# When the attention of a gated mix asks for VectorE time, and when the weight sums of one FFN chunk are formed

## The chip, the cores and the metric

The kernel runs on one core of one Trainium2 chip, with the matmuls on TensorE (PE), sums and products on VectorE (DVE), copies and exponentials on ScalarE (ACT), accumulating transfers issued by GpSimd (POOL) and most other transfers by SyncE (SP). The metric is the device time of one execution in microseconds, lower is better. Times are medians of several executions.

## The reference

```python
def _A_ref(x, wqkv, wo):          # S 2048, D 512, H 32, Dh 16
    W, dil = 8, 2
    qkv = (x @ wqkv).reshape(B, S, 3, H, Dh)           # then split into q, k, v by head
    idx = pos[:, None] - (arange(W) * dil)[None, :]    # eight keys, two apart, none before 0
    logits = where(idx >= 0, einsum(q, k[idx]) * Dh ** -0.5, -1e9)
    return einsum(softmax(logits), v[idx]).reshape(B, S, D) @ wo

def _B_ref(x, w_gate, w_up, w_down):                   # F 1792
    return (gelu(x @ w_gate) * (x @ w_up)) @ w_down

g = sigmoid((x * gate_w).sum(-1, keepdims=True))
return g * _A_ref(x, wqkv, wo) + (1 - g) * _B_ref(x, w_gate, w_up, w_down)
```

All data are float32. A token of even number needs only even tokens for its attention, and one of odd number only odd ones.

## The kernel before

The tokens are handled in two halves by parity, `par` 0 and `par` 1, each of 1024 tokens in eight tiles of 128 (`jj` 0 to 7). Every matrix operand is split into a rounded part and a remainder (`hi`, `lo`), and a product takes three matmuls: high by high, remainder by high, high by remainder.

For a half the stages are: `project(par, 0)` makes the first half of the keys and queries, `project(par, 1)` the values, `ffn(par)` the FFN in `FC` = 14 chunks of 128 hidden channels. For `par` 0 the first projection is written out by hand at the start. The second half of the keys and queries is made inside the first FFN chunks: `project_one(par, jj)` makes one tile (12 matmuls), tiles 0 to 5 in chunk 0, tiles 6 and 7 in chunk 1. From chunk 2 on, a chunk has four tiles of the down projection in the same places (`down`, six matmuls each, for the pair of chunks before); the last pair's eight down tiles stand behind the chunks, in the tail of `ffn`.

A chunk multiplies by a fast scheme with seven products of six matmuls each instead of eight (`product`, L480), on sums of activation blocks (`sums_x`) and sums of weight blocks. The weight sums of chunk f are formed by `combine(f)` on VectorE (three subtractions, L423) in the buffer `raw` that `fetch(f)` filled (`raw` has two buffers). `operands` makes from them, for two groups of products, the two parts: ScalarE writes the negated rounded part (L441), a GpSimd transfer adds the raw value to it in place (L442), and ScalarE writes the rounded part (L446). `down_w` does the same for the down weights (L470, L471, L473). For `par` 1 the parts of the first group come back from DRAM, where `keep` and `keep_parts` stored them. `gate_up` writes out the order of one chunk: steps `idle(0)` to `idle(8)` between its products and the four `pieces`; the dictionary `do` holds what is called at a step, filled by `at(step, function, ...)`, and `late` carries a chunk's last product into the next chunk.

Attention is work for VectorE, 128 channels (a unit `u`, four of them a half) at a time. The generator `attention()` yields the price in us of each step that it has emitted: `scores` (four pairs of a product L288 and a reduction L291, 2.3 each), `softmax`, `mix` (four times a product L326, sums L330 to L334, two transposes L339 that go to DRAM). It is asked by `pull(budget)`: the budget is added to a credit, and steps are emitted while the credit is above zero. So the numbers in the calls of `pull` say how much attention stands beside which matmuls:

```python
def idle(i, n):
    for x in do.get(i, ()):
        x()
    pull(n * PACE[par] * (1.0 if par or f + 1 < FC else 0.8))
```

`PACE` is (0.9, 1.12), and the `n` of a chunk add up to 4.1. Once a unit's softmax is emitted, `attention` looks whether the keys of the next unscored unit are complete (`done`). If so, their load is emitted at once and that unit's scores follow this unit's mix; if not, the next mix follows, and pays a pause of `LOAD` = 4.0 between the load of its values and its first product. Keys, values and products have one buffer each.

The program is written in this order, but the order on each engine is made by a planner that simulates the kernel: each instruction has a priority by its place in the text, attention's is set behind by `BEHIND` = 150 places, and `paced(ins)` makes an instruction wait for the last matmul emitted before it (products of the attention, weight sums and some splits are paced).

The output weights are applied at the end, in `out_first` (half 0) and `finish` (half 1): the last matmuls need the mixed values of half 1's last unit, written to DRAM and read back (L720).

Of the kernel before, what the change touches and what calls it, by code (L numbers as in the profile page):

```python
# [32 lines left out]
PACE = (0.9, 1.12)  # L33
# [11 lines left out]
def tile_gated_mix(ctx: ExitStack, tc: tile.TileContext, xt, wqkv, wff, wo, out):  # L45
# [11 lines left out]
    def tl(tag, dt=F32):  # L57
        return pool.tile([P, COLS.get(tag, 512)], dt, name=tag, bufs=BUFS[tag])
# [5 lines left out]
    def bank(tag):  # L64
        return psum.tile([P, 512], F32, name=tag, bufs=BUFS.get(tag, 1))
# [119 lines left out]
    def qkv_mm(ps, par, jj, cb, kcs, c0=0, cn=512):  # L185
        t = slice((jj % BT) * P, (jj % BT + 1) * P)
        for kc in kcs:
            xh, xl = X[par, jj // BT, kc]
            wh, wl = WC[cb, kc]
            for n, (a, w) in enumerate(((xh, wh), (xl, wh), (xh, wl))):  # L190
                LAST[:] = [nc.tensor.matmul(ps[:, :cn], a[:, t], w[:, c0:c0 + cn], start=(kc == 0 and n == 0),  # L191
                                            stop=(kc == KC - 1 and n == 2))]
# [17 lines left out]
    def take(ps, par, jj, hh, vals, tag=None):  # L210
        st = tl(tag or next(stages))[:, :512]
        n = CU if vals else 512
        nc.scalar.activation(st[:, :n], ps[:, :n], AF.Copy)
        two = st.rearrange("p (a c d) -> p a c d", a=2, c=2)
        dst = VS[par, hh] if vals else KS[par, hh]
        queue = nc.sync if (vals if par else not vals) or hh and not vals else nc.scalar
        queue.dma_start(rows(dst[:, W:], jj), two[:, 0])
        if not vals:
            queue.dma_start(rows(QS[par, hh], jj), two[:, 1])
        elif not hh:  # L220
            nc.scalar.activation(z[:, par, jj:jj + 1], ps[:, CU:CU + 1], AF.Copy)
# [23 lines left out]
    def project_one(par, jj):  # L245

        ps = bank(f"acc{jj % BT}")
        qkv_mm(ps, par, jj, 2, range(KC))
        take(ps, par, jj, 1, False, tag=None if jj < 5 else "c")
        pull((2.7, 2.2)[par])  # L250
        if jj == NP - 1:
            done.add((par, 2))

# [136 lines left out]
    def pull(budget, key=None):  # L390
        credit[0] += budget
        while credit[0] > 0 and (key is None or key not in done):
            with tc.high_priority(offset=-BEHIND):
                c = next(fill, None)
            if c is None:
                credit[0] = 0.0
                return
            credit[0] -= c
        if key:
            credit[0] = 0.0  # L400
# [27 lines left out]
    def operands(par, f, i):  # L428


        n = len(GROUPS[i]) * QW
        w = tl(f"g{i}", F32R)
        hi, lo = w[:, :n], w[:, n:2 * n]
        for k, op in enumerate(GROUPS[i]):
            WG[f, op] = hi[:, k * QW:(k + 1) * QW], lo[:, k * QW:(k + 1) * QW]
        if par and not i:
            nc.sync.dma_start(w[:, :2 * n].bitcast(F32), WS[f, i])
            yield
            return
        raw = RAW[f][:, (0, 4)[i] * QW:][:, :n]  # L440
        nc.scalar.activation(lo, raw, AF.Copy, scale=-1.0)  # L441
        nc.gpsimd.dma_start(lo.bitcast(F32), raw, accum_op=OP.add)  # L442
        if not i:
            KEEP[f] = w[:, :2 * n]
        yield
        ins = nc.scalar.activation(hi, raw, AF.Copy)  # L446
        if f:
            paced(ins)
# [18 lines left out]
    def down_w(f):  # L467
        d = WD[f] = tl("d", F32R)
        rd = RD.pop(f)
        paced(nc.scalar.activation(d[:, 512:], rd, AF.Copy, scale=-1.0))  # L470
        nc.gpsimd.dma_start(d[:, 512:].bitcast(F32), rd, accum_op=OP.add)  # L471
        yield
        paced(nc.scalar.activation(d[:, :512], rd, AF.Copy))  # L473
# [32 lines left out]
    NG = FC // 2  # L506
    out_v = out.rearrange("(p j) d -> j p d", j=NT)

    def down(par, gr, t, b):
        if b == t == gr == 0:  # L510
            ACC.update((t, bank(f"acc{t}")) for t in range(BT))
        pp = bank("p") if b else ACC[t]
        if b and gr:
            nc.scalar.activation(pp, RT[BT + t], AF.Copy)
        ts = slice(t * P, (t + 1) * P)
        for i in range(2):
            hh_, hl_ = Hs[2 * gr + i, b]
            d = WD[2 * gr + i]
            for n, (a, w) in enumerate(((hh_, d[:, :512]), (hh_, d[:, 512:]), (hl_, d[:, :512]))):
                LAST[:] = [nc.tensor.matmul(pp, a[:, ts], w, start=(i == 0 and n == 0 and gr == 0),  # L520
                                            stop=(i == 1 and n == 2), skip_group_check=True)]
        jj = BT * b + t
        if gr == NG - 1 and par:
            nc.scalar.activation(pp, pp, AF.Copy, scale=gc[:, par, jj:jj + 1])
            ACC[jj] = pp
        elif gr == NG - 1:
            st = tl("s")
            nc.scalar.activation(st, pp, AF.Copy, scale=gc[:, par, jj:jj + 1])
            nc.gpsimd.dma_start(out_v[2 * jj], st)
        elif b:  # L530
            if gr == 0:
                RT[BT + t] = tl("rt")
            nc.scalar.activation(RT[BT + t], pp, AF.Copy)  # L533
        if par or gr < NG - 2:
            pull(1.2 * PACE[par])

    def gate_up(par, f, pieces, do):

# [84 lines left out]
    def ffn(par):  # L623
        XOP.update(((n, kc), X[par, blk, kc + k]) for n, blk, k in (("a11", 0, 0), ("a12", 0, 2), ("a22", 1, 2))
                   for kc in range(2))
        todo = iter(())
        for f in range(FC):
            do = {}

            def at(i, x, *args):  # L630
                do.setdefault(i, []).append(lambda: x(*args))

            if f > 1:
                pieces = [[lambda b=b, i=i: down(par, f // 2 - 1, f % 2 * 2 + i, b)] for b in range(2) for i in range(2)]
            else:
                pieces = [[lambda jj=jj: project_one(par, jj) for jj in jjs]
                          for jjs in (((0, 1), (2, 3), (4, 5), ()), ((6,), (7,), (), ()))[f]]
            if f + 1 < FC:
                for i in range(2):
                    steps = operands(par, f + 1, i)  # L640
                    at(1 + 2 * i, next, steps, None)
                    at(5 + i, next, steps, None)
                at(0 if f != 1 else 5, fetch_d, f + 1)
                for g_ in ((), (0, 1))[f] if f < 2 else (f,):
                    steps = down_w(g_)
                    at(2 if f > 2 else 4, next, steps, None)
                    at(7, next, steps, None)
            else:
                steps = down_w(f)
                at(1, next, steps, None)  # L650
                at(4, next, steps, None)
            if par:
                if f + 2 < FC:
                    at(0, fetch_sums, f + 2)
                else:
                    at(0, fetch_o) if f + 2 == FC else None
                if f + 1 == FC:
                    todo = chain(load_o(), channels_of(0, 0))
                    for i in range(1, 9):
                        at(i, next, todo, None)  # L660
            else:
                if f + 2 < FC:
                    at(1, fetch, f + 2)
                    at(8, combine, f + 2)
                else:
                    at(0, fetch_x, 1, f + 2 - FC)
                if f + 1 < FC:
                    do.setdefault(0, []).insert(0, lambda: keep(f + 1))
                at(0, keep_parts, f)
                if f + 2 == FC:  # L670
                    at(8, early)
                if f + 1 == FC:
                    todo = before()
                    for i in range(2, 9):
                        at(i, next, todo, None)
            gate_up(par, f, pieces, do)
        for _ in todo:
            pass
        fourth()
        if par:  # L680
            out_first()
            oT = {}
        for b in range(2):
            for t in range(BT):
                down(par, NG - 1, t, b)
                if par and t == 0:
                    oT[0, b] = channels(par, 0, b)
                if not par and not b:
                    split_kq() if t % 2 else again(0, 1 + t)
                elif not par and b:  # L690
                    again(1, (2, 3, 0, 1)[t])
        if par:
            finish(oT)
# [199 lines left out]
```

## Time and profile before

| | |
|---|---|
| Three executions, us | 614.82, 616.45, 616.71 (median 616.45) |
| Span of the profiled execution, us | 614.2 |
| Profiled execution's own time | not recorded apart from the span; the span lies 0.6 under the fastest of the three and 2.25 under the median |
| Granted TensorE clock | 1.000 |
| TensorE busy, us | 604.1 (98%) |
| Weight loads busy, us | 505.3 (82%) |
| VectorE busy, us | 513.7 (84%) |
| ScalarE busy, us | 376.9 (61%) |
| GpSimd busy, us | 82.5 (13%) |
| DMA | 132.48 MB, mean 216 GB/s |

The profile shows one execution: the page has busy times by engine, a strip of 40 slices, the chain of work that ended last, and groups of instructions by source line. The trace behind it can be asked for the timeline of one engine, for who waited for whom, and for busy times in chosen stretches. Times are in us from the start of the span. In a row of the timeline "x6" merges six equal instructions, and the bracket gives the idle time of the engine before them and what ended it. Matmul ends are modelled, so matmuls in a row overlap in these rows.

By stage: the first projections of half 0 run to about 53 us, FFN 0 to about 297, the projections of half 1 mostly from 287 to 345, FFN 1 and the output from there to the end.

### The profile page before, as it was taken

The page shows a single profiled execution, that of the slowest core. Times are in us where ns is not written, and L with a number is a line of the kernel's source. Part 1 is how long each engine was busy: PE and PEld are TensorE (multiplying, and loading weights), DVE is VectorE, ACT ScalarE, POOL GpSimd, SP SyncE. Part 2 cuts the span into 40 slices and gives each one's busy share as a digit, 9 for nine tenths or more (in the row PEclk, how much of TensorE's full clock was granted, in tenths as well). Part 3 has the DMA queues.
Part 4 walks back from the last instruction along what each step waited for, and adds up shares of the span by engine and source line. Part 5 has one row for each costly group of instructions (what it writes and reads, how often), then busy time and mean ns, then how long its engine had stood idle before and what let it go on. Part 6 is the DMA issues. An engine that isn't in the chain of part 4 may idle for free.

```text
span 614.2 us, 8246 instructions
## 1 busy us (share of the span) xinstructions
PE 604.1 (98%) x2839; PEld 505.3 (82%) x2839; DVE 513.7 (84%) x598; ACT 376.9 (61%) x633; POOL 82.5 (13%) x110
## 2 busy tenths in 40 slices
PE   9999998999999999999999999999999999999997
PEld 7899886877878888888889888888888888888885
DVE  6849699878998888756698998899899889797972
ACT  6554545674867877857356439447756676685632
POOL 0061011120212121101100002101011101101300
PEclk9999999999999999999999999999999999999999
DMA  8398949797889988995639969787888769937724
GB/s 286 98 252 253 319 145 299 192 262 226 204 225 277 305 210 219 280 231 179 237 93 330 305 174 266 210 235 186 238 200 221 162 225 215 268 86 206 91 64 154
DMA packets 85591, 132.48 MB, mean 216 GB/s; under 512 B 8111, under 2 KB 52271, under 8 KB 85550
## 3 DMA queue, kind: packets, MB, share of 16 engines
q1 hardware_dynamic: 63742, 94.27, 46.9%
q0 software_dynamic: 12672, 32.84, 28.1%
q10 hardware_dynamic: 9136, 4.85, 2.6%
q8 instruction: 22, 0.36, 0.3%
q14 instruction: 19, 0.16, 0.1%
HBM read 67.18 MB, written 36.77 MB: 169 GB/s over the span
## 4 chain that ended last, share of the span: by engine, by line
PE 81%; issue 8%; DMA 7%; DVE 3%; ACT 0%; POOL 0%; SPq 0%; POOLq 0%; DVEq 0%; ACTq 0%
PE p L480 35%; PE acc L191 15%; PE acc L520 11%; PE p L520 11%; PE p L742 5%; PE p L191 4%; DMA raw<-wff 3%; PE acc L742 2%; DMA g<-raw 2%; DMA d<-r 1%; DVE prod L326 1%; DMA raw<-xt 1%; DMA ws<-raw 1%; DVE raw L423 0%; DVE prod L330 0%
## 5 line engine op out<-in xcount | busy, mean ns | idle before, releaser
L480 PE MATMUL p<-S,g 128*128 128x512 f32 x672 | 166.6, 389 | 0.8 <-DVE c L490 0.8
L480 PEld LDWEIGHTS p<-S,g 128*128 128x128 f32 x672 | 126.0, 188 | 27.3 <-DVE c L490 1.3
L480 PE MATMUL p<-A,g 128*128 128x512 f32 x504 | 127.4, 390 | 2.9 <-ACT g L446 1.2
L480 PEld LDWEIGHTS p<-A,g 128*128 128x128 f32 x504 | 94.2, 188 | 23.9 <-DMA g<-raw 1.8
L288 DVE TENSOR_TENSOR prod<-kq 128x2048 f32<-128x2048 f32 x32 | 73.1, 2284 | 13.2 <-DMA kq<-kq 5.9
L326 DVE TENSOR_TENSOR prod<-v,lg 128x2048 f32<-128x2048 f32 x32 | 73.0, 2281 | 6.4 <-DMA v<-vs 4.9
L442 POOL DMA_DIRECT2D g<-raw x42 | 36.4, 867 | 298.3 <-ACT g L441 145.5
L291 DVE TENSOR_REDUCE lg<-prod 128x128 f32<-128x2048 f32 x32 | 73.0, 2282 | 0.3
L520 PE MATMUL p<-d,hh 128*128 128x512 f32 x224 | 68.6, 389 | 0.0
L520 PE MATMUL acc<-d,hh 128*128 128x512 f32 x224 | 60.7, 390 | 1.1 <-DMA d<-r 1.1
L520 PEld LDWEIGHTS acc<-d,hh 128*128 128x128 f32 x224 | 42.0, 188 | 10.4 <-DMA d<-r 1.4
L446 ACT ACTIVATE g<-raw 128x1024 fp32r<-128x1024 f32 (+1 forms) x42 | 41.3, 988 | 13.1 <-PE p L480 12.8
L520 PEld LDWEIGHTS p<-d,hh 128*128 128x128 f32 x224 | 42.0, 188 | 8.8
L490 DVE TENSOR_TENSOR c<-p,s 128x512 f32<-128x512 f32 x56 | 38.2, 685 | 12.9 <-PE p L480 12.6
L441 ACT ACTIVATE g<-raw 128x1024 fp32r<-128x1024 f32 (+1 forms) x42 | 41.3, 983 | 9.9 <-DVE raw L423 9.5
L485 ACT ACTIVATE s<-p 128x512 f32<-128x512 f32 x56 | 33.1, 593 | 21.4 <-PE p L480 21.2
L497 DVE TENSOR_TENSOR hl<-c,hh 128x512 fp32r<-128x512 f32 x56 | 38.0, 679 | 9.3 <-ACT hh L496 9.3
L494 DVE TENSOR_TENSOR c<-c 128x512 f32<-128x512 f32 x56 | 38.3, 685 | 8.4 <-ACT c L586 7.9
L520 PE MATMUL p<-d,hl 128*128 128x512 f32 x112 | 42.9, 389 | 0.0
L496 ACT ACTIVATE hh<-c 128x512 fp32r<-128x512 f32 x56 | 35.1, 626 | 9.7 <-DVE c L494 9.2
L533 ACT ACTIVATE rt<-p 128x512 f32<-128x512 f32 x48 | 27.9, 594 | 20.2 <-PE p L520 20.1
L191 PE MATMUL acc<-g,A 128*128 128x258 f32 (+2 forms) x228 | 39.5, 306 | 0.0
(146 smaller groups left out, 912.1 us busy)
## 6 DMA issues: line engine op xcount, KB each, us to landing
g<-raw POOLq DMA_DIRECT2D x28, 512.0 KB, 7.3
raw<-wff SPq DMA_DIRECT2D x42, 256.0 KB, 3.8
ws<-g SPq DMA_DIRECT2D x14, 768.0 KB, 5.5
g<-ws SPq DMA_DIRECT2D x14, 768.0 KB, 6.6
r<-wff SPq DMA_DIRECT2D x28, 256.0 KB, 4.3
d<-r POOLq DMA_DIRECT2D x28, 256.0 KB, 6.4
g<-raw POOLq DMA_DIRECT2D x14, 384.0 KB, 5.9
v<-vs SPq DMA_DIRECT2D x8, 512.0 KB, 7.7
```

The costliest lines, as they stand in the source:

```text
L191: LAST[:] = [nc.tensor.matmul(ps[:, :cn], a[:, t], w[:, c0:c0 + cn], start=(kc == 0 and n == 0), stop=(kc == KC - 1 and n == 2))]
L288: paced(nc.vector.tensor_tensor(prod, spans(k, jj), q[:, jj:jj + 2, None, :].to_broadcast([P, 2, W, UC]), op=OP.mult))
L291: nc.vector.tensor_reduce(two_of(lg, jj), prod.rearrange("p j w (h d) -> p (j w) h d", d=DH), axis=AX.X, op=OP.add)
L326: paced(nc.vector.tensor_tensor(prod.rearrange("p j w (h d) -> p (j w) h d", d=DH), spans(v, jj).rearrange("p j w (h d) -> p j w h d", d=D ...
L441: nc.scalar.activation(lo, raw, AF.Copy, scale=-1.0)
L446: ins = nc.scalar.activation(hi, raw, AF.Copy)
L480: LAST[:] = [nc.tensor.matmul(ps, w_, a_, start=(start and kc == 0 and n == 0), stop=(kc == 1 and n == 2), skip_group_check=True)]
L490: nc.vector.tensor_tensor(c, ps, s, op=OP.add)
L494: nc.vector.tensor_tensor(ge, ge, up, op=OP.mult)
L497: nc.vector.tensor_tensor(hl_, ge, hh_.bitcast(F32), op=OP.subtract)
L520: LAST[:] = [nc.tensor.matmul(pp, a[:, ts], w, start=(i == 0 and n == 0 and gr == 0), stop=(i == 1 and n == 2), skip_group_check=True)]
L742: LAST[:] = [nc.tensor.matmul(pa, a, b, start=(first and n == 0), stop=(last and n == 2), skip_group_check=True)]
```

## The change

Three edits. `project_one` asks for attention only in the second half; in the first half its eight calls no longer add 2.7 each to the credit. `down` asks for 1.2 * `PACE` in every pair of chunks; before, the first half's last two pairs (the down tiles in chunks 12 and 13, and the eight in the tail) asked for nothing. And in chunk 0 of the first half `combine(2)` is called at step 6, ahead of the third piece and the product of that step, instead of at step 8.

```diff
@@ project_one
-        pull((2.7, 2.2)[par])
+        if par:
+            pull(2.2)
         if jj == NP - 1:
             done.add((par, 2))
@@ down
-        if par or gr < NG - 2:
-            pull(1.2 * PACE[par])
+        pull(1.2 * PACE[par])
@@ ffn
                 if f + 2 < FC:
                     at(1, fetch, f + 2)
-                    at(8, combine, f + 2)
+                    at(8 if f else 6, combine, f + 2)
```

No instruction is added or removed; what changes is where attention's steps and chunk 2's weight sums stand in the program.

## The prediction

> **What bounds the kernel now.** I read the page's totals first, then the list of what TensorE waited for, then the timeline around each of these waits, then the table of busy time by stage.
>
> ```profile
> span 614.2 us, 8246 instructions
> PE 604.1 (98%) x2839; PEld 505.3 (82%) x2839; DVE 513.7 (84%) x598; ACT 376.9 (61%) x633; POOL 82.5 (13%) x110
> ...
> PE p L480 <- DVE c L490: 1.6, 2, 0.8
> PE p L480 <- ACT g L446: 1.2, 1, 1.2
> PE acc L520 <- DMA d<-r: 1.1, 1, 1.1
> ...
> PE p L480 <- DMA g<-raw: 1.0, 2, 0.5
> ```
>
> TensorE is busy for 604.1 of 614.2 us. Its list of waits holds only six matmul waits inside the kernel's body, and the timeline shows that all lie in the first FFN:
>
> ```profile
> 75.58 1.52 PE L480 MATMUL p<-S,g 128*128 128x512 f32 x6
> ...
> 93.25 1.66 PE L480 MATMUL p<-A,g 128*128 128x512 f32 x6 [1.19 <-ACT g L446]
> 96.33 0.50 PE L520 MATMUL acc<-d,hh 128*128 128x512 f32 x1 [1.11 <-DMA d<-r]
> 129.89 3.01 PE L480 MATMUL p<-S,g 128*128 128x512 f32 x12 [0.84 <-DVE c L490]
> 133.82 2.58 PE L480 MATMUL p<-A,g 128*128 128x512 f32 x10 [0.46 <-DMA g<-raw]
> 143.28 1.66 PE L480 MATMUL p<-A,g 128*128 128x512 f32 x6 [0.76 <-DVE c L490]
> 176.53 1.65 PE L480 MATMUL p<-A,g 128*128 128x512 f32 x6 [0.52 <-DMA g<-raw]
> ...
> 422.69 6.80 PE p L480 x30
> ...
> 605.44 1.07 PE L742 MATMUL p<-S,hh 128*128 128x512 f32 x4
> ```
>
> The idle times add up to 4.88 us. A stall costs more than its idle time. In the chain of waits 30 matmuls take 6.80 us, 0.227 each, so six started back to back take 1.36 us from first start to next start; the timeline counts the last one to its modelled end, 1.52 us for six (the row at 75.58). So 0.16 us of the lost time ahead of each stall is counted as busy, and the six after a stall take 1.66 instead of 1.52. With 0.30 us for each, the six stalls cost 4.88 + 1.80 = 6.7 us. This is all that any change in the order of the work can win inside the body; everything else is matmuls back to back.
>
> Who makes TensorE wait? VectorE, in two of the stalls by name and in the first two by way of ScalarE:
>
> ```profile
> 57.18 9.04 DMA raw<-wff
> ...
> 79.81 2.28 DVE L288 TENSOR_TENSOR prod<-kq 128x2048 f32<-128x2048 f32 x1
> ...
> 82.61 0.68 DVE L423 TENSOR_TENSOR raw<-raw 128x512 f32<-128x512 f32 x1
> 83.21 2.28 DVE L291 TENSOR_REDUCE lg<-prod 128x128 f32<-128x2048 f32 x1
> 85.41 0.41 DVE L423 TENSOR_TENSOR raw<-raw 128x256 f32<-128x256 f32 x1
> 85.74 2.28 DVE L288 TENSOR_TENSOR prod<-kq 128x2048 f32<-128x2048 f32 x1
> 85.85 0.85 ACT L441 ACTIVATE g<-raw 128x768 fp32r<-128x768 f32 x1 [4.04 <-DVE raw L423]
> 87.94 0.42 DVE L423 TENSOR_TENSOR raw<-raw 128x256 f32<-128x256 f32 x1
> 88.39 1.06 ACT L441 ACTIVATE g<-raw 128x1024 fp32r<-128x1024 f32 x1 [0.72 <-DVE raw L423]
> 90.31 1.15 ACT L470 ACTIVATE d<-r 128x512 fp32r<-128x512 f32 x2
> 91.23 1.74 POOL L471 DMA_DIRECT2D d<-r  x2 [0.63 <-ACT d L470]
> 92.35 1.79 ACT L446 ACTIVATE g<-raw 128x768 fp32r<-128x768 f32 x2
> ```
>
> Chunk 2's raw weights had landed at 66.2 (the chain's transfer: 57.18 + 9.04). Their three sums (L423) ran at 82.61, 85.41 and 87.94, with an attention step of 2.28 us ahead of each. ScalarE, which runs in order, waited 4.04 + 0.72 us for them, and everything behind was late by that: the split L441, the down weights L470, whose accumulating transfer left at 91.23 and ended the second stall at 96.33, and L446, which ended the first.
>
> By stage:
>
> ```profile
> 79.00:94.00 15.00, 13.81 (x61) 11.16 (x60) 15.00 (x14) 8.17 (x14) 3.45 (x4) 1.00 0.52 136
> ...
> 230.00:245.00 15.00, 15.00 (x68) 12.43 (x67) 13.78 (x18) 10.90 (x17) 2.66 (x4) 1.00 0.86 217
> 260.00:298.00 38.00, 38.00 (x170) 31.44 (x169) 20.84 (x33) 20.91 (x37) 3.08 (x5) 1.00 0.73 215
> 298.00:345.00 47.00, 47.00 (x298) 42.64 (x297) 44.17 (x54) 26.77 (x59) 3.92 (x6) 1.00 0.75 230
> ```
>
> The columns are length, then busy time of PE, weight load, DVE, ACT and POOL. Where VectorE has 13.78 us of work in 15, TensorE loses nothing; where it is full (79 to 94), TensorE loses 1.2. And from 260 to 298 VectorE has 20.84 us of work in 38.
>
> **The change, part by part.** *The request that goes.* Eight calls of `project_one` in FFN 0 no longer ask for 2.7 us of attention each: 21.6 us less in chunks 0 and 1. Walking the credit through the generator by hand: before, attention was handed out by the end of chunk 1 up to the third product of the first mix; now it has reached the third product of the second unit's scores. That is 21.6 us by the credit's prices, close to the 22 us that these steps last. What stays in the two chunks is the usual 4.1 x 0.9 = 3.7 us each. Of the attention steps of 2.28 us that stand between the sums, at most one is left in this window (three products or reductions are now handed out in the two chunks), so VectorE has about 15.0 - 4 x 2.28 = 6 us of work there, 4 to 8. The sums then wait for no attention step, ScalarE's 4.76 us of waiting go, and the transfer of the down weights (issued 91.23, used 96.33) has 4.76 us where 1.11 were missing. Both stalls go: 1.19 + 1.11 + 0.60 = 2.9 us. The stalls at 129.89, 133.82 and 143.28 lie in the backlog that these requests built: 0.84 + 0.46 + 0.76 + 0.90 = 3.0 us. From chunk 2 on a chunk asks for 3.7 + 4 x 1.08 = 8.0 us of attention as before, and the window 230 to 245, which has that same demand without a backlog, shows no loss. I take these 3.0 us as gone too (bounds: 0 to 3.0).
>
> *A wait that moves.* One cause of the stall at 143.28 is seen on VectorE:
>
> ```profile
> 139.73 2.29 DVE L326 TENSOR_TENSOR prod<-v,lg 128x2048 f32<-128x2048 f32 x1 [4.93 <-DMA v<-vs]
> ```
>
> Unit 1's values are loaded into the only `v` buffer once unit 0's mix has left it, and the two mixes followed each other, because unit 2's keys were not complete at the choice. With attention later, that choice falls in chunk 3, the keys are there, and unit 2's scores come between. But the whole sequence is now one unit of scores ahead, so units 2 and 3 of this half mix back to back, in the projections of the second half, with the pause of 4.0 in credit. I expect a wait of up to 4.93 us there. TensorE's projections are evacuated by ScalarE, so I charge none of it now and keep 1.06 us (what the stall at 143.28 lost) for the range.
>
> *The sums sooner.* `combine(2)` stands at step 6 instead of 8, two projection tiles and one product (30 matmuls, 6.8 us) earlier. The raw weights have landed by then. Its 0.68 + 0.41 + 0.42 = 1.5 us now stand ahead of the sum c22 on VectorE, whose bank is next needed by the chunk's last product, which runs in the following chunk: nothing. SP's write of the same sums, behind which the key and query stores and the key loads are queued, can only get earlier. Bounds: 0 to 2.9 us, already counted above; it secures them.
>
> *The request that comes.* Chunks 12 and 13 and the eight last down tiles ask for 16 x 1.08 = 17.3 us. From 260 to 298 VectorE has 38 - 20.84 = 17.2 us free: it just fits, with no margin, and the stage behind has 47.0 - 44.17 = 2.8 us free. The hand-offs here are tight:
>
> ```profile
> 285.91 0.88 DVE L594 CAST A<-raw 128x512 fp32r<-128x512 f32 x2 [4.26 <-PE acc L520]
> 287.30 1.28 DVE L87 TENSOR_TENSOR A<-raw,A 128x512 fp32r<-128x512 f32 x2
> ...
> 287.06 2.43 PE L191 MATMUL acc<-g,A 128*128 128x512 f32 x10
> ```
>
> The first of the two L87 is done near 287.94; the fifth matmul, which may be the first to need it, starts at 287.06 + 4 x 0.227 = 287.97. The 4.26 us of idle VectorE before the cast will now hold attention steps of 2.28 us that can't be interrupted. The order on each engine is planned with this load known, and down tiles are there as other work for TensorE, so I take half a step, 1.1 us, lost here (bounds: 0, and four such hand-offs x 2.28 = 9.1).
>
> *The end.* In sum, attention is asked for 21.6 - 17.3 = 4.3 us less in this half, and the pause of 4.0 keeps it that late until the last unit.
>
> ```profile
> 566.38 0.69 DVE L494 TENSOR_TENSOR c<-c 128x512 f32<-128x512 f32 x1 [2.04 <-ACT c L586]
> 568.33 0.69 DVE L307 TENSOR_REDUCE m<-lg 128x64 f32<-128x512 f32 x1 [1.25 <-ACT lg L306]
> ...
> 594.37 0.71 DVE L339 STREAM_TRANSPOSE tb<-o 128x512 f32<-128x512 f32 x1
> ...
> 601.59 0.69 DVE L87 TENSOR_TENSOR hl<-raw,hh 128x512 fp32r<-128x512 f32 x1 [6.50 <-ACT hh L86]
> ```
>
> The last transposed block is followed by its way through DRAM; its split is done at 602.28 and first used at 605.44: 3.16 us of margin. A lateness of 4.0 would cost 0.84 us; but VectorE idled 2.04 + 1.25 us around the softmax before it, which can take some of it up. I take 0.3 (bounds 0 to 0.84).
>
> *What remains.* The stall at 176.53 waits for an accumulating transfer in a stage with the usual load; one like it, 0.52 + 0.30 = 0.8 us, may come in any chunk. I keep 0.8.
>
> Sum: -6.7 + 0.8 + 1.1 + 0.3 = -4.5 us. The profiled span of 614.2 becomes 609.7. Around the span lies what separates it from the measured times (614.82 to 616.71, median 616.45), 2.25 us at the median; it stays. 616.45 - 4.5 = 612.0 us (611.95 rounded).
>
> **The rivals.** *Slower: attention in the last two chunks delays the splits of the second half.* For it: the demand of 17.3 us meets 17.2 us free, the split above is used 0.03 us after it stands, and the moved wait of up to 4.93 us comes right behind. Against: from 275 to 298 TensorE has tiles of two kinds to choose from. It decides from the point where the hand-offs lose more than the 6.7 us won; at all four, 9.1 us, and 1.06 for the moved wait, the time is 616.45 - 6.7 + 10.2 = 620.0 us.
>
> *No change: VectorE is the bound.* The requests are moved, not removed; if 513.7 us of VectorE set the pace, the stalls would only move with the backlog, into chunks 2 to 9 and the end: 616.45. For it: the full window at 79. Against: VectorE is idle for 100 us, 17 of them where the requests go. The Trainium skill's page "Perfetto Trace Analysis", section "Identifying the Most-Contended Engine", leans to this rival: it calls matmul busy time a bad measure and judges TensorE's headroom by the busy share of weight loads, for VectorE by occupancy. By that rule VectorE (84%) would be above TensorE (82%), and the sum would be zero. The trace does not bear it out: in windows with no TensorE idle at all the weight loads are busy for 12.43 of 15.00 us, the same 83%, so 82% is what a full TensorE shows here.
>
> *The planner undoes it.* The sums are placed by a planner, and may stay where they were; then only the attention steps' absence helps, the first stall stays (1.19 + 0.30), and the time is 612.0 + 1.5 = 613.5.
>
> **How the numbers follow.** A measurement of this kernel can tell about 0.3% (1.85 us) from no change: 614.6 to 618.3 counts as the same. Forecast, 612.0, with its own range of 609.8 (all 6.7 us won, nothing lost) to 614.5 (chunks 3 and 4 give only half, 1.5, and the second half's start costs 1.1 more): 0.60. The planner's rival, 613.5: 0.07. No change, 616.45: 0.15. Slower, 620.0: 0.18. So faster 0.67, same 0.15, slower 0.18. The range runs from 609.8 to 618.5: it takes in the forecast and the case of no change and leaves out the slower one.
>
> **What would show it.** Right: TensorE's list of waits has no ScalarE L446 and no d<-r entry; L423 of chunk 2 stands before 78 with no attention step between its parts; VectorE's busy time from 79 to 94 falls to 4 to 8 us and from 260 to 298 rises above 35; the wait of L326 for v<-vs leaves 139 and reappears after 300. Wrong: TensorE idle between 275 and 345 of more than 2 us, by the casts L594 or the splits L87; idle before the last L742 matmuls, ended by hl; or stalls by L490 again between 100 and 180.

## The result, and the profile after

| | median, us | spread, us | runs |
|---|---|---|---|
| before, same chip | 615.21 | 613.42 to 616.71 | 5 |
| after | 611.79 | 610.94 to 614.49 | 5 |

The ratio is 0.9954, interval 0.9932 to 0.9976: about 2.8 us faster, between 1.5 and 4.2. Run again in a later comparison it was 0.9961 (0.9945 to 0.9977), 2.4 us. Ratios are used below, since the kernel before had medians between 614.32 and 615.43 in the comparisons. The profiled spans are 614.2 and 610.4 us.

From line 251 to about 535 the changed kernel's line numbers are one higher (L480 is L481). Its totals and its list of what TensorE waited for:

```profile
span 610.4 us, 8251 instructions
PE 602.1 (99%) x2839; PEld 503.6 (83%) x2839; DVE 515.0 (84%) x598; ACT 380.0 (62%) x635; POOL 82.8 (14%) x110
```

```profile
...
PE p L481 <- DMA g<-raw: 0.7, 1, 0.7
PE p L521 <- ACT p L515: 0.6, 1, 0.6
PE p L191 <- DVE A L84: 0.5, 1, 0.5
PE acc L521 <- DMA d<-r: 0.3, 1, 0.3
```

This L191, and a wait of 1.0 us by L72 that is not shown, lie at the start. The other three are the body's, and the timeline places them at 92, 195 and 374 us, the last in FFN 1:

```profile
92.16 0.50 PE L521 MATMUL acc<-d,hh 128*128 128x512 f32 x1 [0.33 <-DMA d<-r]
195.03 0.73 PE L521 MATMUL p<-d,hh 128*128 128x512 f32 x2 [0.56 <-ACT p L515]
373.90 1.20 PE L481 MATMUL p<-A,g 128*128 128x512 f32 x4 [0.71 <-DMA g<-raw]
```

Idle time in the body is 1.60 us instead of 4.88, and no entry names ScalarE's L447 (L446 before) or VectorE's L491 (L490 before). How chunk 2's weights came sooner is seen on VectorE and on the engines that follow it:

```profile
69.13 0.68 DVE L424 TENSOR_TENSOR raw<-raw 128x512 f32<-128x512 f32 x1
...
72.67 2.29 DVE L289 TENSOR_TENSOR prod<-kq 128x2048 f32<-128x2048 f32 x1 [2.25 <-DMA kq<-qs]
74.88 0.42 DVE L424 TENSOR_TENSOR raw<-raw 128x256 f32<-128x256 f32 x1
75.33 0.85 ACT L442 ACTIVATE g<-raw 128x768 fp32r<-128x768 f32 x1 [2.98 <-DVE raw L424]
75.82 2.28 DVE L292 TENSOR_REDUCE lg<-prod 128x128 f32<-128x2048 f32 x1
78.02 0.42 DVE L424 TENSOR_TENSOR raw<-raw 128x256 f32<-128x256 f32 x1
...
87.66 1.74 POOL L472 DMA_DIRECT2D d<-r  x2 [1.26 <-ACT d L471]
```

The sums start at 69.13, 74.88 and 78.02 (before 82.61, 85.41, 87.94), with an attention step still ahead of the second and of the third. The accumulating transfer of the down weights leaves at 87.66 instead of 91.23, and of the 1.11 us that it lacked 0.33 are left.

The windows of the changed kernel (length, then PE, weight load, DVE, ACT, POOL):

```profile
79.00:94.00 15.00, 14.67 (x65) 11.82 (x64) 12.34 (x11) 9.28 (x15) 2.60 (x3) 1.00 0.85 224
260.00:298.00 38.00, 38.00 (x177) 31.58 (x176) 33.83 (x48) 24.75 (x42) 5.49 (x9) 1.00 0.64 201
298.00:345.00 47.00, 47.00 (x290) 42.39 (x289) 42.74 (x55) 23.59 (x54) 1.76 (x2) 1.00 0.86 247
```

VectorE gained 13.0 us of work from 260 to 298, and TensorE shows no idle time there, as before.

Where the span went, by the spacing of TensorE's matmuls (what lies between two starts beyond the usual 0.227 us counts as lost): the body loses 3.4 us less (in FFN 0 1.9 instead of 6.6; in FFN 1 1.15 where nothing was lost), the end costs 1.3 us more, and 1.8 us come from the start and do not belong to the change:

```profile
8.67 1.76 PE L191 MATMUL acc<-g,A 128*128 128x512 f32 x4
10.27 0.62 PE L191 MATMUL p<-g,rt 128*128 128x512 f32 x2
```

This is the kernel before; in the changed one the second group starts at 8.48, and in a second trace of the kernel before at 8.74. So of the 3.9 us between the profiled spans 2.1 are the change's, near the 2.4 to 2.8 of the many runs.

The end of the changed kernel:

```profile
594.73 0.71 DVE L340 STREAM_TRANSPOSE tb<-o 128x512 f32<-128x512 f32 x1
...
602.15 0.69 DVE L87 TENSOR_TENSOR hl<-raw,hh 128x512 fp32r<-128x512 f32 x1 [3.09 <-ACT hh L86]
602.24 2.03 PE L742 MATMUL p<-S,hh 128*128 128x512 f32 x8
604.11 1.07 PE L742 MATMUL p<-S,hl 128*128 128x512 f32 x4
604.53 1.10 ACT L788 ACTIVATE s<-p 128x512 f32<-128x512 f32 x2 [1.93 <-PE p L742]
...
606.57 0.40 SPq L790 DMA_DIRECT2D out<-r  x1
```

and of the kernel before:

```profile
609.98 0.39 PE L742 MATMUL p<-S,hl 128*128 128x512 f32 x1
611.27 0.33 SPq L790 DMA_DIRECT2D out<-r  x1
```

The last transposed block stands about as early as before (594.73 against 594.37), but TensorE is done with the rest sooner, so the block is only 10.4 us ahead of its last matmul instead of 16. Its split ends at 602.84, and TensorE does not wait: it runs the last eight high parts first and then four remainders in a row. Thus four output tiles end within 1.07 us instead of one after the other; their copies and stores pile up, and the span ends 5.20 us after the last matmul instead of 3.87.

### The profile page after: what moved, and what is told of

Read it like the earlier page. It is cut to its first block, busy times and chain, and to the rows that moved or that the text cites. A ratio compares the mean times of both kernels' runs of the same rounds, so it can differ in the third digit from the quotient of the medians.

```text
span 610.4 us, 8251 instructions
## 1 busy us (share of the span) xinstructions
PE 602.1 (99%) x2839; PEld 503.6 (83%) x2839; DVE 515.0 (84%) x598; ACT 380.0 (62%) x635; POOL 82.8 (14%) x110
## 4 chain that ended last, share of the span: by engine, by line
PE 93%; DMA 3%; issue 1%; DVE 1%; ACT 1%; POOL 0%; SPq 0%; POOLq 0%; ACTq 0%
PE p L481 40%; PE acc L191 18%; PE p L521 12%; PE acc L521 12%; PE p L742 5%; PE p L191 4%; PE acc L742 2%; DMA g<-raw 2%; DMA d<-r 1%; DMA raw<-xt 1%; DVE prod L327 0%; ACT g L442 0%; POOL g L443 0%; ACT s L788 0%; ACT lg L307 0%
## 5 line engine op out<-in xcount | busy, mean ns | idle before, releaser
L481 PE MATMUL p<-S,g 128*128 128x512 f32 x672 | 165.7, 389 | 0.0
L481 PEld LDWEIGHTS p<-S,g 128*128 128x128 f32 x672 | 126.1, 188 | 26.2
L481 PE MATMUL p<-A,g 128*128 128x512 f32 x504 | 127.5, 390 | 0.7 <-DMA g<-raw 0.7
L481 PEld LDWEIGHTS p<-A,g 128*128 128x128 f32 x504 | 94.3, 188 | 21.0 <-DMA g<-raw 1.1
L447 ACT ACTIVATE g<-raw 128x1024 fp32r<-128x1024 f32 (+1 forms) x42 | 41.1, 987 | 9.6 <-PE p L481 9.4
L491 DVE TENSOR_TENSOR c<-p,s 128x512 f32<-128x512 f32 x56 | 38.1, 686 | 10.0 <-PE p L481 10.0
L331 DVE TENSOR_TENSOR prod<-prod 128x1024 f32<-128x1024 f32 x32 | 39.0, 1220 | 0.4
```

Of the source, the lines that this page charges most:

```text
L331: nc.vector.tensor_tensor(prod[:, :, :4], prod[:, :, :4], prod[:, :, 4:], op=OP.add)
L481: LAST[:] = [nc.tensor.matmul(ps, w_, a_, start=(start and kc == 0 and n == 0), stop=(kc == 1 and n == 2), skip_group_check=True)]
```

## The experiments

The theory: VectorE, which runs in order, carried too much attention beside the first chunks of FFN 0, and this delayed the weight sums and the chunk products; moved to the end of the half, that work finds VectorE free. First rival: the two requests cancel, and the sums placed sooner do it alone. Second rival: VectorE's total is the bound, and what one stage wins another gives back.

**Only the request taken away** (kernel before with the first edit alone).

```diff
-        pull((2.7, 2.2)[par])
+        if par:
+            pull(2.2)
```

> The change's first part alone: project_one asks for no attention in the first half; the last two chunks still ask for nothing and the sums stay at step 8. Theory 1 (the requests beside project_one build a VectorE backlog that holds up TensorE in chunks 1 to 4; what is not asked for in the first half comes late at the end): the six stalls of FFN 0 shrink from 6.7 us to under 3, but 21.6 us of attention are missing at the end, where 3 us of margin stand against it: TensorE idles 10 to 20 us in the last matmuls, time 622 to 632. Theory 2 (the gain comes from the earlier sums alone): FFN 0 keeps its stalls at chunk 2, time over 625. Theory 3 (VectorE's total sets the pace, the place of the requests does not matter): 615, no change.

639.49 us, ratio 1.0389 (1.0353 to 1.0425), 24 us slower. TensorE's waits:

```profile
PE p L743 <- ACT hh L86: 8.3, 1, 8.3
PE acc L743 <- ACT hh L86: 5.6, 1, 5.6
PE acc L191 <- ACT z L221: 3.2, 1, 3.2
PE acc L521 <- DMA d<-r: 2.1, 2, 1.2
```

21.6 us of attention that nobody asks for come out at the end: the last two transposed blocks stand at 607.08 and 620.45, and the last matmuls wait 5.6 and 8.3 us for their ways back. So the new request in the last two chunks is what makes the first edit possible. The size was missed. Behind each of these two waits TensorE's granted clock is halved (0.50, the third number from the end), which the expectation did not count:

```profile
628.00:634.00 6.00, 5.49 (x12) 3.80 (x12) 1.38 (x2) 1.39 (x3) 0.00 (x0) 0.50 0.04 14
```

It is 0.50 from 614 to 619 too. The 24 matmuls there start 0.43 us apart instead of 0.227, about 4.8 us more in all. By the spacing 5.9 us are lost in the projections of the second half as well, where one wait takes 3.2. The d<-r stall of 1.2 us at chunk 2 is still there.

**Both requests, sums left late** (changed kernel, one edit undone).

```diff
-                    at(8 if f else 6, combine, f + 2)
+                    at(8, combine, f + 2)
```

> Both attention edits, the sums back at step 8 of chunk 0. Theory 1: with no attention step between them the sums are early enough either way; time 611.5 to 613, within 1 us of the changed kernel, no wait of TensorE for L447 in chunk 2. Theory 2 (the earlier sums make the gain): 615, the wait of about 1.2 us at the first product of chunk 2 is back.

614.01 us, ratio 0.9979 (0.9961 to 0.9998). The timeline of VectorE, ScalarE and TensorE around chunk 2:

```profile
80.65 0.68 DVE L424 TENSOR_TENSOR raw<-raw 128x512 f32<-128x512 f32 x1
81.25 2.28 DVE L292 TENSOR_REDUCE lg<-prod 128x128 f32<-128x2048 f32 x1
83.44 0.87 DVE L424 TENSOR_TENSOR raw<-raw 128x256 f32<-128x256 f32 x2
83.89 0.85 ACT L442 ACTIVATE g<-raw 128x768 fp32r<-128x768 f32 x1 [3.83 <-DVE raw L424]
93.63 0.50 PE L521 MATMUL acc<-d,hh 128*128 128x512 f32 x1 [1.21 <-DMA d<-r]
```

The sums are 2 to 4 us sooner than before, through attention alone. ScalarE's stall of 1.2 us (L446 before) has shrunk to 0.2; that of d<-r is back in full. So the sums' place is worth a stall of its own. The time lies between those of the two theories.

**Only the sums sooner** (kernel before).

```diff
-                    at(8, combine, f + 2)
+                    at(8 if f else 6, combine, f + 2)
```

> The third part alone: the sums at step 6, attention asked for as before. Theory 1: the attention steps still stand ahead of the sums on VectorE; some of the first two stalls (2.9 us) may go, the three at 129 to 143 stay; 613.5 to 615.2. Theory 2: 611.8, all of the change's gain.

614.06 us, ratio 0.9977 (0.9953 to 1.0002): not told apart from nothing, nor from the attention edits alone (0.9979), nor from the whole change. Single times reach from 610.2 to 617.3. The profiled execution, with a span of 609.05, is the second fastest of twelve: its trace shows what the sums do in a fast execution, and not what the slower ones lose.

```profile
79.00:94.00 15.00, 14.64 (x65) 11.78 (x64) 14.93 (x12) 9.21 (x15) 2.60 (x3) 1.00 0.81 211
92.70 0.50 PE L520 MATMUL acc<-d,hh 128*128 128x512 f32 x1 [0.36 <-DMA d<-r]
139.40 3.19 PE L480 MATMUL p<-A,g 128*128 128x512 f32 x12 [0.39 <-DVE c L490]
```

VectorE is as full from 79 to 94 as before (14.93 of 15 us), and yet the stall by L446 is gone and that of d<-r is down to 0.36: the three sums start at 69.64, 74.91 and 78.05, as early as in the changed kernel. Behind chunk 2 one stall of the backlog is left, 0.39 us at 139.

**Half the request left in place** (changed kernel).

```diff
-        if par:
-            pull(2.2)
+        pull((1.35, 2.2)[par])
```

> The changed kernel with half the request beside project_one in the first half (1.35 instead of 0 or 2.7 for each of eight calls, 10.8 us). Theory 1: a dose in between: stalls of 1.5 to 4 us in chunks 1 to 4 of FFN 0; attention is less late at the end, so the last outputs are not held up (0.5 to 1.3 us better there): 611 to 613.5. Theory 3: 615.

614.16 us, ratio 0.9984 (0.9960 to 1.0008): the time is a miss, and the ratio is told apart neither from nothing nor from the changed kernel's. In its profiled execution the losses are spread (this kernel has the line numbers of the kernel before, to line 533):

```profile
PE p L480 <- DMA g<-raw: 1.6, 1, 1.6
PE acc L520 <- DMA d<-r: 0.9, 3, 0.4
```

The three for d<-r are 0.21 us at chunk 2, 0.36 in the backlog at 111 and 0.29 in FFN 1; the largest stall, at 173.9, waits for an accumulating transfer in a later chunk, and whether half the request causes it is open. Here the end after the last matmul is 3.85 us.

**The changed kernel again.**

> The changed kernel once more, beside the three below. Theory 1 (both parts count: the earlier sums take away the stalls at chunk 2, the missing requests those of chunks 3 and 4 and the exposure to late transfers): 611 to 612.5, ratio 0.993 to 0.997, single times spread over less than 4 us; the last matmuls of three or four tiles end together and 5 us lie between the last matmul and the end of the span. Theory 3 (order noise of the planner, not the parts): no different from the two single parts, 613 to 614.5.

612.89 us, ratio 0.9961 (0.9945 to 0.9977), span 611.17; 5.19 us lie behind the last matmul, as in the first trace and with the sums late. So the longer end belongs to the change, and to its attention edits. The single times reach from 611.0 to 616.2, more than the 4 us expected.

**The kernel before again**, one execution with a profile.

> The kernel before once more, for a second trace. If the first trace is typical: six stalls of 6 to 7 us in FFN 0 at the same places. If the stalls hang on the time that transfers take: other sizes and places, 3 to 9 us in all, and matmul starts at the very beginning that differ by 1 to 2 us.

613.84 us, span 612.05. Its waits in the body:

```profile
PE p L480 <- DVE c L490: 1.3, 2, 0.8
PE acc L520 <- DMA d<-r: 1.1, 1, 1.1
PE p L480 <- ACT g L446: 0.9, 1, 0.9
PE p L480 <- DMA g<-raw: 0.2, 1, 0.2
```

The stalls at chunk 2 and those by L490 come again; the g<-raw ones differ between executions. There are five stalls instead of six, and FFN 0 loses 5.3 us by the spacing instead of 6.6. VectorE's wait for `v` comes again too, 4.41 us at 137.

**More attention per matmul in the second half**, so that it ends sooner (changed kernel).

```diff
-PACE = (0.9, 1.12)
+PACE = (0.9, 1.16)
```

> The changed kernel with PACE 1.16 instead of 1.12 in the second half: about 5 us more attention asked for over FFN 1, so that the last unit is no longer late. If the late last unit costs the 1.3 us by which the end after the last matmul grew: that end shrinks from 5.2 to about 3.9 us and the time falls by 1 us to 610 to 611. If the end is not worth that, or VectorE falls behind in FFN 1: 611.5 to 613.

612.23 us, ratio 0.9950 (0.9933 to 0.9967), beside 0.9961 for the changed kernel in the same comparison: not told apart. The end is back at 3.85 us, but FFN 1 loses 2.8 us by the spacing, beside 2.0 in the changed kernel's trace of this comparison.

**No pause before a mix** (changed kernel). This pause exists for the wait for `v`.

```diff
-            yield from mix(*un, LOAD if mixed else 0.0)
+            yield from mix(*un, 0.0)
```

> The changed kernel without the pause of 4.0 in credit that a mix pays when it follows a mix. If this pause makes the end late: the last transpose comes 3 to 5 us earlier against the last matmul, the end after the last matmul shrinks to 3.9 us, time 610 to 611. If the pause had hidden the load of the values: VectorE waits up to 5 us for v<-vs near 315, with TensorE losing up to 1.1 us: 611.5 to 613.

611.06 us, ratio 0.9926 (0.9911 to 0.9942), beside 0.9961 in the same comparison: 2.2 us better, and the two intervals do not meet. From the end of its timeline:

```profile
589.35 0.71 DVE L340 STREAM_TRANSPOSE tb<-o 128x512 f32<-128x512 f32 x1
...
604.95 0.39 PE L742 MATMUL p<-S,hl 128*128 128x512 f32 x1
```

The last transpose is 5.4 us earlier, the last tile ends alone, the tail is 3.86 us, and the stall at 373.9 is gone. Nothing on VectorE waits for `v`.

**The same with the sums late.**

```diff
-            yield from mix(*un, LOAD if mixed else 0.0)
+            yield from mix(*un, 0.0)
...
-                    at(8 if f else 6, combine, f + 2)
+                    at(8, combine, f + 2)
```

> The kernel of e6 (both attention edits, no pause) with the sums back at step 8. Theory 1 (the earlier sums are worth their own 1 to 2 us at chunk 2, whatever the end does): the stall of about 1.2 us for d<-r at chunk 2 is back, time 612 to 613, ratio 0.995 to 0.997. If the requests alone do it and the sums only secure it: 611, as e6.

612.74 us, ratio 0.9965 (0.9944 to 0.9986): 2.4 us worse by the ratios than with the sums soon, which ran in another comparison; the intervals (from 0.9944, to 0.9942) just do not meet. The d<-r stall of chunk 2 is back, the first of TensorE's waits in the body:

```profile
PE acc L521 <- DMA d<-r: 1.6, 2, 1.2
```

**No pause, and the sums at step 6 in every chunk of the first half.**

```diff
-            yield from mix(*un, LOAD if mixed else 0.0)
+            yield from mix(*un, 0.0)
...
-                    at(8 if f else 6, combine, f + 2)
+                    at(6, combine, f + 2)
```

> The kernel of e6 with the sums at step 6 in every chunk of the first half, not in chunk 0 alone. If late sums still cost something in the later chunks (0.56 us of TensorE's waits are left in FFN 0 near 195, and transfers g<-raw land late): 609.5 to 610.8. If chunk 0 was the only place where they were late: 611, and the earlier sums may hold up c22 (L491) in a full VectorE, 611 to 613.

609.22 us, ratio 0.9915 (0.9886 to 0.9945): 5.2 us under the kernel before, the best version here. Its totals, and all that TensorE waited for behind the start:

```profile
span 607.5 us, 8241 instructions
PE 601.3 (99%) x2839; PEld 504.1 (83%) x2839; DVE 512.1 (84%) x598; ACT 380.7 (63%) x636; POOL 83.1 (14%) x110
```

```profile
...
PE acc L521 <- DMA d<-r: 0.3, 1, 0.3
```

One stall of 0.3 us is left in the body. VectorE does the same work (512.1 us) as in the slower kernels. Beside 0.9926 for the missing pause alone, the share of the sums in the other chunks is not told apart.

**The sums at step 6 in every chunk, attention as before** (kernel before).

```diff
-                    at(8, combine, f + 2)
+                    at(6, combine, f + 2)
```

> The kernel before with the sums at step 6 in every chunk of the first half; attention is asked for as before, project_one included. If the sums' place is what counts and the requests hardly matter: the stalls of FFN 0 fall below 1.5 us, time 609.5 to 611.5, near the kernel of e8. If the requests count on their own (their backlog on VectorE holds up L491's work and leaves no room for late transfers): stalls of 1.5 us or more between 100 and 180 remain, 612 to 614, single times spread over more than 4 us.

614.29 us, ratio 0.9989 (0.9970 to 1.0008): nothing that can be told. The profiled execution is the fastest of twelve, which reach to 617.1. Its two largest waits in the body:

```profile
PE acc L520 <- DMA d<-r: 1.6, 2, 1.3
PE p L480 <- DVE c L490: 0.7, 1, 0.7
```

Of the wait for d<-r 0.26 us are left at chunk 2; the other 1.35, at 112, and the wait for L490, at 141, lie in the backlog. So sums that are called sooner free TensorE at chunk 2 even while attention fills VectorE, but not in the chunks behind it.

**The best version again.**

> The kernel of e8 once more, beside the other: 609 to 610, ratio 0.989 to 0.995.

609.87 us, ratio 0.9916 (0.9892 to 0.9940). This ran in the same comparison as the kernel just above, with the sums in the same places; the requests and the pause are the difference, 0.9916 against 0.9989, and the intervals do not meet. Of these 4.5 us the pause alone was worth 2.2 above. So the first rival, the sums alone, falls. The interval also lies under that of the changed kernel's second comparison (0.9945 to 0.9977), and overlaps that of its first (0.9932 to 0.9976).

**What all the traces show together.** Idle time of TensorE in us, one profiled execution per trace:

| sums of chunk 2 | attention beside `project_one` in the first half | traces | chunk 2, by L446 (L447) | chunk 2, by d<-r | 100 to 190 us |
|---|---|---|---|---|---|
| step 8 | as before | 2 | 1.19, 0.88 | 1.11, 1.11 | 2.58, 1.50 |
| step 8 | none | 3 | 0.16 to 0.29 | 1.18 to 1.22 | 0 |
| step 6 | as before | 2 | 0 | 0.36, 0.26 | 0.39, 2.07 |
| step 6 | half | 1 | 0 | 0.21 | 2.38 |
| step 6 | none | 6 | 0 | 0.24 to 0.34 | 0 |

The d<-r stall at chunk 2 goes with the place of the sums, whatever attention does. The stalls from 100 to 190 go with the request, whatever the sums do. The L446 stall shrinks by either. So the attention edits and the sums' place take away different stalls, and each alone has a ratio of 0.998 (0.9979 and 0.9977), about half the gain; with the sums sooner in every chunk it was 0.9989.

## Why the prediction was right, and where its steps failed

The forecast of 612.0 us was met (611.79); the range of 609.8 to 618.5 took in no change as well, so that lying inside it says little. Its mechanism, attention that delays the first FFN's weights and products, is shown for the stalls from 100 to 190: they are gone in all nine traces without the request, and there in all five with it, whole or half. For the two stalls at chunk 2 it was right only in part. And terms of opposite sign were missed, so that the closeness of the sum is in part luck.

*The two stalls at chunk 2* went as priced: 0.33 us remain of 2.30. How was wrong twice. The step "at most one attention step is left, VectorE 4 to 8 us" failed: VectorE is busy for 12.34 us from 79 to 94, and between 72 and 95 six attention steps run instead of eight. The credit says how much attention is emitted beside which matmuls, not when it runs; a step is held by the matmul emitted before it, and the planner runs chunk products ahead, so attention steps come as early as their matmul (this is read from the program; no run tests it by itself). And "already counted, it secures them" failed: the attention edits alone leave the d<-r stall whole (1.21 us with the sums late), and the sums alone take both stalls but 0.26 to 0.36 us, with VectorE full. The sums' place is worth 1.1 to 2.4 us by the ratios of the two pairs (0.9979 to 0.9961 or 0.9954; 0.9965 to 0.9926), near the 1.21 + 0.30 of the stall; the first pair's intervals overlap, the second's just do not meet. The prediction priced it at nothing and the attention edits at all of it: right in the sum, wrong in the shares. The rival that the planner undoes it is answered by the sums at 69.13 to 78.02.

*The three stalls at 129 to 143* are gone, and none like them came: as predicted. The sums alone left 0.39 and 0.72 us there in their two traces, where the two of the kernel before have 2.06 and 1.50, so a part of this too may be theirs.

*The wait that moves* did not reappear; VectorE's list of waits has no entry for `v` any more. Units 2 and 3 did mix back to back; the step that failed is the wait of up to 4.93 us, and with it the range's 1.06:

```profile
308.78 0.34 SPq L273 DMA_DIRECT2D v<-vs  x1
...
318.00 2.25 DVE L327 TENSOR_TENSOR prod<-v,lg 128x2048 f32<-128x2048 f32 x1
```

This load of the changed kernel has two parts, which land at 312.6 and 315.1. Until 318.00 VectorE is busy without a gap, with unit 2's last sums and the second half's activation sums, so the load is hidden; the stage from 298 to 345 has TensorE at 47.00 of 47. Without the pause there is no such wait either; in the best version there is one of 1.8 us at 319, beside which TensorE loses nothing. So the pause of 4.0 buys nothing here.

*The start of the second half* was charged 1.1 us (0 to 9.1) and cost nothing. VectorE rose to 33.83 us there, not above 35, and TensorE was busy for 38.00 of 38. The slower rival falls at this point: the request in these chunks costs nothing there, and without it the kernel is 24 us slower.

*The end* was charged 0.3 us with an upper bound of 0.84, and cost 1.3: outside the bounds. I had counted margin before the first use of the last split, and TensorE indeed does not wait for it (0.36 us in the second trace); but a late split makes it finish four tiles together, and four copies and stores in a row are then the end. Two changes that make attention earlier by different means, more of it per matmul and no pause, bring back 3.85 and 3.86 us, so lateness is the cause.

*What remains* was put at 0.8 us. By the matmuls' spacing FFN 0 loses 1.9, FFN 1 1.15 and the projections 0.1, 3.1 together; the stall at 373.9 was not foreseen. It comes again in the second trace (0.55) and with the sums late (1.19), and is absent in the three traces without the pause and with the sums soon; but with neither the pause nor the sums soon 0.58 us stand at 377. Its cause stays open.

Together: -6.6 + 3.1 + 0 + 1.3 = -2.2 us, beside the 2.4 to 2.8 measured. The forecast of -4.5 was too large; it was met within 0.2 us because it started from a median of 616.45, where the kernel before had 614.32 to 615.43 in all later comparisons.

*VectorE as the bound* falls. The trace has the same VectorE total after (515.0 against 513.7) and the time fell; the best version holds 84% too. The Trainium skill, "Perfetto Trace Analysis", section "Identifying the Most-Contended Engine", would read TensorE's headroom from MFU (its arithmetic as a share of the peak) and from the busy share of the weight loads; that share stayed at 82 to 83% whether TensorE had 4.88 us of stalls in the body or 0.3, so here it does not show the headroom. What did was the list of what each engine waited for.

Open: whether half the request really gives back most of the gain (0.9984, with an interval that takes in 1 and the changed kernel's ratio); what the sums sooner are worth without the attention edits (0.9977 and 0.9989, both with intervals that include 1), although the traces of both show chunk 2 freed; and what the slower executions of these three kernels lose, whose times spread over 4.5 to 7 us.

## What to carry to other kernels

When an in-order engine carries both background work and the first link of a chain (here sums on VectorE, split on ScalarE, accumulating transfer), take the background work out of the stage where that chain is tight, and give it back in a stage with idle time on that engine before it is needed; taking it out without giving it back cost 24 us here. Move the chain's first link ahead as well: here the two took away different stalls, and each alone gave a ratio of 0.998, about half the gain and hardly told from nothing. Then look at the end again, since lateness can appear there as outputs that finish together, with no wait of the busiest engine to show it.

## What the runs showed of the hardware that was not expected

The first matmuls can differ between executions of the same program: with the kernel before, the group at the start began at 10.27 us in one trace and at 8.74 in another; the four matmuls ahead of it take 1.76 us in the one and 1.09 in the other:

```profile
7.81 1.09 PE L191 MATMUL acc<-g,A 128*128 128x512 f32 x4
8.74 0.62 PE L191 MATMUL p<-g,rt 128*128 128x512 f32 x2
```

That is 1.5 us between two executions, as much as one of the edits is worth; a single pair of spans does not settle a change of this size.

A wait near the end can cost more than its length: after 5.6 and 8.3 us of idle TensorE (the kernel with only the request taken away) the granted clock was 0.50 for the 12 matmuls behind each wait.
